# Attention with eight heads on two halves of the partitions, and the decay moved from the queries to the rows of the product

## The chip, the core and the metric

The kernel runs on one core of a Trainium2 chip. The core has a matrix engine (TensorE, in the profile PE, with its weight loads as PEld), a vector engine (VectorE, DVE), a scalar engine for functions (ScalarE, ACT), a general engine (GpSimd, POOL) and a queue that issues transfers (SyncE, SP). Matrix products are written to PSUM, eight banks of 512 float32 for each of the 128 partitions; everything else lives in SBUF. The metric is the device time of one execution in microseconds; lower is better. Times of a kernel differ between executions, so a median of several runs stands for it.

## What is computed

Two stages follow each other: a recurrent attention (mLSTM) with 4 batches, 8 heads, 768 steps and 40 values a head, and then a gated two-layer network over the 320 values of all heads, whose gate mixes the 768 positions.

```python
# attention; C, n and m start empty
m_new = max(f_gate[t] + m, i_gate[t])
f_stab, i_stab = exp(f_gate[t] + m - m_new), exp(i_gate[t] - m_new)
C = f_stab * C + i_stab * outer(v[t], k[t])
n = f_stab * n + i_stab * k[t]
y[t] = sigmoid(o_gate[t]) * (C @ q[t]) / max(abs(n @ q[t]), 1)
# network over x = all heads of y, 320 wide
h = max(x @ w_in, 0); u, v = halves of h (512 each)
v_s = w_spatial @ layer_norm(v) + b_spatial   # over the 768 positions
out = (u * v_s) @ w_out
```

## The kernel before

The 768 steps of a batch are cut into six blocks of 128 steps, and a block into two chunks of 64 (e = 0 and 1). There are 24 blocks in all, numbered n. Within a chunk the recurrence is written as products of matrices: keys and queries give scores, which are multiplied by a matrix of decays W and then by the values; what comes from earlier chunks is a state (40 x 41 a head: C and, as the 41st column, n) that meets the queries, times the decay since the chunk's start.

*The gates* (`gates`, L125 to L168) are done in two halves of 384 steps, on 32 partitions (4 x 8). Sums of gates go to DRAM (`scr_g`, `scr_a`, L141), and so does the decay since the chunk's start, `scr_e` (L161 to L165). They come back with the block's loads: `GM` and `AT`, whose product `ex` (L398) gives the exponents of W, and `Eb` (L378 to L381), the decay broadcast over 40 partitions.

*A block* has three parts. `att_load(n)` issues its loads on SP's queue: keys and queries `QK` (two transfers, L350 to L352; even chunk on partitions 64 to 103, odd on 0 to 39), `GM`, two of `Eb`, and two of `RH` (values, keys and output gates by time). `att1(n)` makes `ex`, the scores `s` (L361: for each head one product of 40 x 64 by 40 x 64 a chunk), W (ScalarE, L403), the product of scores and W into `KS` (VectorE, one instruction a chunk, L406), the queries times the decay, also into `KS` (GpSimd, L411, 40 x 512 a chunk), and the keys times the last column of W (GpSimd, L417). `att2(n)` makes the state's increments `dc` (L430, L432), carries the state from chunk to chunk with four VectorE instructions (L442 to L448; the state lies in rows of `RH` beside the values, alternately on the lower and the upper partitions), and then `pv` (L455, L456): one product a head and chunk whose 104 or 128 rows hold scores and decayed queries in one operand, and values and state in the other. VectorE divides and applies the output gate (L458 to L467), TensorE transposes (L476), and ScalarE and VectorE split the result into two float32r parts `xH` and `xL` (L478 to L481). A block's `att2` stands behind the `att1` of the next block and the loads of the one after.

*The network* follows: `a_v` (L494) makes v and its norm, `b_u` (L540) makes u (`pu`), mixes the positions (`pb`) and multiplies (GpSimd, L560), `c_out` (L565) writes the output. Weights come as float64 words and are split by `cvt` (L201), mostly on VectorE, and that for the first batch runs beside its attention. `seq` in line 54 is the written order of that first part: a token such as `q2` issues the loads of keys and queries of block 2, `s2` makes its scores, `h0` and `h1` are the halves of the gates, `A0` the loads of block 0, `T0` its `att1`, each `S` a block's attention, `C` a conversion. In later batches four or two steps of attention are placed between the `b_u` of each half (L633 to L644). From this order a scheduler, which simulates the engines, makes each engine's instruction stream; it places TensorE's work of other parts where it expects a wait.

PSUM is divided by kind (L90): `s` (two banks, `ex` and the scores), `dc`, `pv` and `px` (one each) and `pm` (three; `pu`, `pb`, `pc` and `a_v`).

## Time and profile before

| | us |
|---|---|
| median of 3 runs | 459.68 |
| lowest and highest run | 452.23, 465.68 |
| profiled execution, first to last instruction (span) | 441.9 |
| GpSimd busy in it | 173.6 |
| ScalarE busy in it | 156.1 |

The profiled execution has no time of its own beside its span. The runs' times include what lies before the first and after the last instruction; the median is 17.8 us above the span, the lowest run 10.3.

A row of a group of instructions reads: line, engine, operation, output from inputs by the program's names, shapes (for a matrix product rows*columns of the stationary operand, then the moving one), how many; then busy time in us and the mean of one in ns; then the engine's idle time just before them and what ended it. A float32 product shows as two records of TensorE, a float32r one as one. PEclk is the share of full speed that TensorE's clock was granted. A row of the timeline begins with the start and the duration, both in us, and merges neighbours of one kind. A row of a stage has the stage, its length, and the busy time of PE, PEld, DVE, ACT and POOL with the number of instructions.

### The profile page before, as it was taken

What the parts mean: (1) busy time and instruction counts of PE and PEld (TensorE: products, weight loads), DVE (VectorE), ACT (ScalarE), POOL (GpSimd) and SP (SyncE); (2) the same over time, 40 slices, a digit from 0 to 9 for tenths busy, and PEclk for the clock granted to TensorE, in tenths of its full rate; (3) what the DMA queues carried; (4) which work ended last, traced back from release to release, by engine and by line L of the source; (5) the groups of instructions that cost most, each with busy time, mean ns of one, the idle gap of its engine ahead of it and who ended that gap; (6) DMA issues with size and microseconds to landing.
All of it is one profiled execution on the core that took longest, in us unless ns stands there. A gap on an engine that the chain in (4) does not pass through costs nothing.

```text
span 441.9 us, 9266 instructions
## 1 busy us (share of the span) xinstructions
PE 402.6 (91%) x3648; PEld 331.9 (75%) x3648; DVE 249.8 (57%) x532; ACT 156.1 (35%) x372; POOL 173.6 (39%) x180
## 2 busy tenths in 40 slices
PE   3459969999898899999999997999999999999996
PEld 3337646678696788977888886677889887799895
DVE  6189967897899985234325465743355664322121
ACT  3144324547333242255422221267112315722211
POOL 4066541577654443236324033465242301633010
PEclk9999999988988998999999996999999999999999
DMA  7975428354055474000302242320024000000101
GB/s 182 201 207 178 133 51 234 110 137 106 20 171 143 113 196 136 0 15 16 91 1 60 93 107 77 92 60 31 30 61 130 8 3 0 32 15 1 45 0 47
DMA packets 18412, 36.83 MB, mean 83 GB/s; under 512 B 4176, under 2 KB 9040, under 8 KB 18368
## 3 DMA queue, kind: packets, MB, share of 16 engines
q1 hardware_dynamic: 14448, 31.43, 26.1%
q10 hardware_dynamic: 3504, 4.03, 2.6%
q0 software_dynamic: 416, 0.76, 0.9%
q8 instruction: 29, 0.48, 0.5%
q14 instruction: 15, 0.12, 0.1%
HBM read 31.79 MB, written 4.42 MB: 82 GB/s over the span
## 4 chain that ended last, share of the span: by engine, by line
PE 71%; DVE 12%; DMA 10%; issue 3%; ACT 2%; SPq 1%; POOL 1%; ACTq 0%; DVEq 0%; POOLq 0%
PE pu L547 12%; PE pb L553 9%; PE pb L555 7%; PE pb L554 7%; PE pv L456 4%; PE pc L571 4%; PE s L361 3%; PE pv L455 3%; PE pc L573 3%; DMA QK<-in_qk 3%; PE pc L572 3%; DMA RH<-in_vk 3%; DMA scr_g<-gp 2%; PE px L476 2%; DVE x L467 1%
## 5 line engine op out<-in xcount | busy, mean ns | idle before, releaser
L411 POOL TENSOR_TENSOR KS<-QK,Eb 40x512 f32<-40x512 f32 x44 | 59.2, 1345 | 69.5 <-DMA Eb<-scr_e 31.3
L560 POOL TENSOR_TENSOR g<-g,u 128x384 f32<-128x384 f32 x32 | 32.6, 1023 | 104.6 <-DVE g L559 89.0
L553 PE MATMUL pb<-wsH,vH 128*128 128x384 f32 x192 | 70.1, 365 | 3.4 <-ACT u L549 2.1
L554 PE MATMUL pb<-wsL,vH 128*128 128x384 f32 x192 | 66.0, 344 | 0.0
L555 PE MATMUL pb<-wsH,vL 128*128 128x384 f32 x192 | 65.9, 346 | 0.0
L361 PE MATMUL s<-QK 40*64 40x64 f32 x768 | 42.8, 255 | 13.3 <-DMA QK<-in_qk 9.7
L361 PEld LDWEIGHTS s<-QK 40*64 40x64 f32 x768 | 34.7, 162 | 22.8 <-DMA QK<-in_qk 10.8
L559 DVE TENSOR_TENSOR g<-pb,bsp 128x384 f32<-128x384 f32 x32 | 17.7, 556 | 53.3 <-PE pb L555 53.0
L553 PEld LDWEIGHTS pb<-wsH,vH 128*128 128x128 f32 x192 | 37.3, 194 | 9.2 <-issue 4.8
L455 PE MATMUL pv<-RH,KS 104*64 104x41 f32 (+1 forms) x384 | 40.1, 247 | 0.4 <-DVE x L465 0.4
L532 POOL TENSOR_TENSOR vL<-v,vH 128x512 fp32r<-128x512 f32 x24 | 31.0, 1292 | 20.8 <-DVE v L531 15.2
L456 PE MATMUL pv<-RH,KS 128*64 128x41 f32 x384 | 37.8, 246 | 1.2 <-DVE RH L443 0.6
L554 PEld LDWEIGHTS pb<-wsL,vH 128*128 128x128 f32 x192 | 37.5, 195 | 0.1
L555 PEld LDWEIGHTS pb<-wsH,vL 128*128 128x128 f32 x192 | 37.1, 194 | 0.2
L549 ACT ACTIVATE u<-pu 128x384 f32<-128x384 f32 x32 | 15.7, 489 | 60.9 <-PE pu L547 53.2
L547 PE MATMUL pu<-xH,wiL 128*128 128x384 f32 (+1 forms) x96 | 36.6, 382 | 0.0
L456 PEld LDWEIGHTS pv<-RH,KS 128*64 128x64 f32 x384 | 30.1, 150 | 8.1 <-issue 3.3
L455 PEld LDWEIGHTS pv<-RH,KS 104*64 104x64 f32 (+1 forms) x384 | 31.0, 150 | 6.7 <-issue 3.2
L547 PE MATMUL pu<-xH,wiH 128*128 128x384 f32 x96 | 34.9, 363 | 0.3 <-ACT ot L575 0.3
L406 DVE TENSOR_TENSOR KS<-s,W 64x512 f32<-64x512 f32 x48 | 32.9, 686 | 2.8 <-PE s L361 1.2
L562 DVE TENSOR_TENSOR big<-g,big 128x384 fp32r<-128x384 f32 x32 | 19.3, 605 | 25.9 <-ACT big L561 25.8
L413 ACT ACTIVATE RH<-RH 128x320 f32<-128x320 f32 x24 | 11.3, 470 | 61.2 <-DMA RH<-in_vk 57.5
(326 smaller groups left out, 863.7 us busy)
## 6 DMA issues: line engine op xcount, KB each, us to landing
RH<-in_vk SPq DMA_DIRECT2D x48, 242.0 KB
QK<-in_qk SPq DMA_DIRECT2D x48, 160.0 KB
Eb<-scr_e SPq DMA_DIRECT2D x48, 80.0 KB
out<-ot ACTq DMA_DIRECT2D x24, 160.0 KB
big<-in_w_sp SPq DMA_DIRECT2D x12, 192.0 KB
w<-in_w_in SPq DMA_DIRECT2D x8, 256.0 KB
w<-in_w_out SPq DMA_DIRECT2D x4, 320.0 KB
w<-in_w_rem SPq DMA_DIRECT2D x2, 256.0 KB
```

The lines of the kernel that those rows point to most:

```text
L361: nc.tensor.matmul(s[64 - p0:128 - p0, h], QK[p0:p0 + D, 0, h], QK[p0:p0 + D, 1, h], start=True, stop=True)
L406: nc.vector.tensor_tensor(out=ks[r, e], in0=s[r], in1=W[r], op=ALU.mult)
L411: eng(K["q" + "eo"[e] + ("0" if b == 0 else "")]).tensor_tensor(out=ks[r, e], in0=QK[r, 1], in1=Eb[r], op=ALU.mult)
L455: nc.tensor.matmul(pv[0:64, h], ks[0:ke, 0, h], v0[0:ke, h], start=True, stop=True)
L456: nc.tensor.matmul(pv[64:128, h], ks[:, 1, h], v1[:, h], start=True, stop=True)
L532: marks["v%d" % (b * NB + k)] = eng(K["vl0"] if b == 0 else K["vl"]).tensor_tensor(out=vL, in0=v, in1=vH.bitcast(F32), op=ALU.subtract)
L547: nc.tensor.matmul(pu, w, x, start=i == 0, stop=i == len(terms) - 1)
L553: nc.tensor.matmul(pb, vH[:, cd], wsH[hf][:, s], start=s == 0, stop=False)
L554: nc.tensor.matmul(pb, vH[:, cd], wsL[hf][:, s], start=False, stop=False)
L555: nc.tensor.matmul(pb, vL[:, cd], wsH[hf][:, s], start=False, stop=s == NB - 1)
L560: marks["m%d" % ((b * 2 + hf) * 4 + d)] = nc.gpsimd.tensor_tensor(out=g, in0=g, in1=u, op=ALU.mult)
L562: marks["g%d" % ((b * 2 + hf) * 4 + d)] = nc.vector.tensor_tensor(out=gL, in0=g, in1=gH.bitcast(F32), op=ALU.subtract)
```

## The change

Heads 0 to 3 now have keys and queries on partitions 0 to 39 and heads 4 to 7 on 64 to 103, both chunks each, in four buffers (`QKS`). The scores of a block use all four 64x64 quarters of the array in turn (`TILES`), in one PSUM buffer of two banks; `KS` is written by one VectorE instruction over 128 partitions. The decayed queries and `Eb` are gone. Scores times values (`XI`, 64 rows) and raw queries times state (`XD`, 40 rows, again over the four quarters) are separate products. The second is multiplied by the decay of its row (`ET`) and added to the first, by two VectorE instructions, before the division. The state has buffers of its own (`ST`), four heads on each half of the partitions, so a step is 104 x 164 in place of 40 x 328; in a batch's first block a buffer of zeros stands for it. `dc` shares the two banks of `XD` with the state's product.

The gates give `ET` (decay by time, through three TensorE transposes a half) and `DEC` (the chunk's whole decay on all partitions, through a product with a loaded matrix `pick`); `scr_e` is gone. `RH` is one transfer a block. `ex` and `px` move to the three banks `pm`. In `seq`, `id` goes ahead of `h0`, and `q3`, `s3` and `rh` are dropped. `keep_warm`, which was called with counts of zero, and choices among engines that were fixed are removed.

```diff
-    'seq': ('h0', 'id', 'q0', 'gm0', 'ks', 'q1', 's0:v1', 's1', 'q2', 'q3', 'at0', 'rh', 's2', 's3', 'La', 'h1', 'A0', ...
+    'seq': ('id', 'h0', 'q0', 'gm0', 'ks', 'q1', 's0:v1', 's1', 'q2', 'at0', 's2', 'La', 'h1', 'A0', ...
...
+    BANKS = {"s": 1, "pm": 3}
 
     def bank(shape, name, kind):
-        tag, n = cfg[kind]
-        t = ps.tile(shape, F32, name=name, tag=tag, bufs=n)
-        return t
+        return ps.tile(shape, F32, name=name, tag=kind, bufs=BANKS[kind])
...
+    ET = const.tile([128, NB, BH], F32, name="ET")
+    DEC = const.tile([128, 2 * NB, 16], F32, name="DEC")
+    pick = const.tile([128, 144], F32, name="pick")[0:BH]
...
+        nc.gpsimd.dma_start(out=pick, in_=a["pick"])
...
-            gv = gz.rearrange("p (k e t) -> p k e t", e=2, t=L)
-            ev = ez.rearrange("p (k e t) -> p k e t", e=2, t=L)
-            for e in range(2):
-                nc.scalar.activation(out=ev[:, :, e], in_=gv[:, :, 1 - e], func=AF.Exp)
-            eng(K["dqg"]).dma_start(out=scr_e[cs].rearrange("c p t -> p c t"), in_=ez.rearrange("p (c t) -> p c t", t=L))
+            nc.scalar.activation(out=ez, in_=gz, func=AF.Exp)
+
+            pe = bank([128, 512], "pe", "pm")
+            for i in range(NB // 2):
+                nc.tensor.transpose(pe[:, i * BH:(i + 1) * BH], ez[:, i * 128:(i + 1) * 128], ident[0:BH, 0:BH])
+            nc.vector.tensor_copy(out=ET[:, z * 3:z * 3 + 3], in_=pe[:, 0:3 * BH].rearrange("p (k c) -> p k c", c=BH))
+            dg = wk.tile([128, NB, 16], F32, name="dg", tag="dg", bufs=1)[0:BH]
+            nc.vector.tensor_tensor(
+                out=dg, in0=ez.rearrange("p (c t) -> p c t", t=L)[:, :, L - 1:L].broadcast_to([BH, NB, 16]),
+                in1=pick[:, 0:16].unsqueeze(1).broadcast_to([BH, NB, 16]), op=ALU.mult)
+            pd = bank([128, 512], "pd", "pm")[:, 0:NB * 16]
+            nc.tensor.matmul(pd, pick[:, 16:144], dg.rearrange("p c x -> p (c x)"), start=True, stop=True)
+            nc.vector.tensor_copy(out=DEC[:, cs], in_=pd.rearrange("p (c x) -> p c x", x=16))
...
+    NKS, NRH, NQK, NST = 3, 3, 4, 4
     VW, KW = H * E, H * D
-    KS = [const.tile([128, 2, H, L], F32, name=f"KS{j}") for j in range(NKS)]
-    RH = [const.tile([128, 2 * VW + 2 * KW], F32, name=f"RH{j}") for j in range(NRH)]
-
-    def rh_v(t, e):
-        o = e * (VW + 2 * KW)
-        return t[:, o:o + VW].rearrange("p (h d) -> p h d", h=H)
+    HH = H // 2
+    HI = 64 + D
...
+    KS = [const.tile([128, H, L], F32, name=f"KS{j}") for j in range(NKS)]
+    RH = [const.tile([128, VW + 2 * KW], F32, name=f"RH{j}") for j in range(NRH)]
+    QKS = [const.tile([128, 2, 2, HH, L], F32, name=f"QK{j}") for j in range(NQK)]
+    ZS = const.tile([128, HH, E], F32, name="ZS")
+    XI = ps.tile([128, 512], F32, name="XI", tag="XI", bufs=1)
+    ST = [const.tile([128, HH, E], F32, name=f"ST{j}") for j in range(NST)]
+    XD = ps.tile([128, 2, 512], F32, name="XD", tag="XD", bufs=1)
+
+    def rh_v(t):
+        return t[:, 0:VW].rearrange("p (h d) -> p h d", h=H)
...
+    def xv(hf):
+        return XD[:, hf, 0:HH * E].rearrange("p (h d) -> p h d", h=HH)
+
+    def dcv(e):
+        return XD[:, e, HH * E:2 * HH * E].rearrange("p (h d) -> p h d", h=HH)
...
-        for t in KS:
-            nc.gpsimd.memset(t[32:64, 1], 0.0)
-
-    def init_rh():
-        for t in RH:
-            nc.gpsimd.memset(rh_v(t, 1)[32:64], 0.0)
+        nc.gpsimd.memset(ZS, 0.0)
+        nc.vector.memset(XD[32:64], 0.0)
...
-        if 2 <= n < K["npre"]:
-            QK = early_keys.tile([128, 2, H, L], F32, name="QK%d" % n)
-        else:
-            QK = ld.tile([128, 2, H, L], F32, name="QK", tag="QK", bufs=2)
-        for e, p0 in ((0, 64), (1, 0)):
-            loads["a%d" % n] = (nc.scalar if n < K["npre"] and K["qkq"] else nc.sync).dma_start(out=QK[p0:p0 + D], in_=a["qk"][b, k, e])
+        QK = QKS[n % NQK]
+        for hf in range(2):
+            loads["a%d" % n] = nc.sync.dma_start(out=QK[64 * hf:64 * hf + D].rearrange("p e w h t -> p (e w h t)"), in_=a["qk"][b, k, hf])
...
+    TILES = ((0, 0), (1, 1), (0, 1), (1, 0))
...
+        s = bank([128, 2, 512], "s", "s")
+        for j in range(HH):
+            for hf, e in TILES:
+                r = slice(64 * hf, 64 * hf + D)
                 nc.tensor.matmul(
-                    s[64 - p0:128 - p0, h], QK[p0:p0 + D, 0, h], QK[p0:p0 + D, 1, h], start=True, stop=True)
+                    s[64 * e:64 * e + 64, hf, j * L:(j + 1) * L], QK[r, e, 0, j], QK[r, e, 1, j], start=True, stop=True)
         sc[n] = s
...
-        Eb = ld.tile([128, H, L], F32, name="Eb", tag="Eb")
-        for e in range(2):
-            nc.sync.dma_start(
-                out=Eb[64 * e:64 * e + D], in_=scr_e[2 * k + e, b * H:(b + 1) * H].unsqueeze(0).broadcast_to([D, H, L]))
         rh = RH[n % NRH]
-        for e in range(2):
-            nc.sync.dma_start(out=rh[64 * e:64 * e + 64, e * VW:e * VW + VW + 2 * KW], in_=a["vk"][b, k, e])
-        tl[n] = (QK, gm, Eb, rh)
+        nc.sync.dma_start(out=rh, in_=a["vk"][b, k])
+        tl[n] = (QK, gm, rh)
...
+        ex = bank([128, H * L], "ex", "pm")
...
-        nc.scalar.activation(out=W, in_=ex, func=AF.Exp)
-        for e in range(2):
-            r = slice(64 * e, 64 * e + 64)
-            nc.vector.tensor_tensor(out=ks[r, e], in0=s[r], in1=W[r], op=ALU.mult)
-        for e, p0 in ((0, 64), (1, 0)):
-            if k == 0 and e == 0:
-                continue
-            r = slice(p0, p0 + D)
-            eng(K["q" + "eo"[e] + ("0" if b == 0 else "")]).tensor_tensor(out=ks[r, e], in0=QK[r, 1], in1=Eb[r], op=ALU.mult)
+        nc.scalar.activation(out=W.rearrange("p h t -> p (h t)"), in_=ex, func=AF.Exp)
+        nc.vector.tensor_tensor(
+            out=ks.rearrange("p (g h) t -> p g (h t)", g=2), in0=s[:, :, 0:HH * L], in1=W.rearrange("p (g h) t -> p g (h t)", g=2), op=ALU.mult)
...
+        kt, v = rh_k(rh), rh_v(rh)
+        s0, s1, s2 = (ST[(2 * n + i) % NST] for i in range(3))
+        if k == 0:
+            s0 = ZS
...
-        dc = bank([128, H, E], "dc", "dc")
+        for e in range(1 if last else 2):
+            r = slice(64 * e, 64 * e + 64)
+            for j in range(HH):
+                for hf in range(2):
+                    h = hf * HH + j
+                    nc.tensor.matmul(dcv(e)[64 * hf:64 * hf + D, j], kt[r, h], v[r, h], start=True, stop=True)
+
+        def step(e, old, new):
+            if old is None:
+                nc.vector.tensor_copy(out=new[0:HI], in_=dcv(e)[0:HI])
+                return
+            tmp = wk.tile([128, HH, E], F32, name="tmp", tag="tmp", bufs=K["tmp"])
+            nc.vector.tensor_tensor(out=tmp[0:HI], in0=old[0:HI], in1=DEC[0:HI, 2 * k + e, b * HH:(b + 1) * HH].unsqueeze(2).broadcast_to([HI, HH, E]), op=ALU.mult)
+            nc.vector.tensor_tensor(out=new[0:HI], in0=dcv(e)[0:HI], in1=tmp[0:HI], op=ALU.add)
+
+        step(0, s0 if k else None, s1)
+        if not last:
+            step(1, s1, s2)
+
+        def inter(e, h):
+            hf, j = divmod(h, HH)
+            r = slice(64 * hf, 64 * hf + D)
+            nc.tensor.matmul(xv(hf)[64 * e:64 * e + 64, j], QK[r, e, 1, j], (s1 if e else s0)[r, j], start=True, stop=True)
+
+        xi = XI[:, 0:H * E].rearrange("p (h d) -> p h d", h=H)
         for h in range(H):
-            nc.tensor.matmul(dc[0:D, h], kt[0:64, h], v0[0:64, h], start=True, stop=True)
-            if not last:
-                nc.tensor.matmul(dc[64:64 + D, h], kt[64:128, h], v1[64:128, h], start=True, stop=True)
-        lo, hi = slice(0, D), slice(64, 64 + D)
-
-        def decay(r):
-            return Eb[r, :, L - 1:L].broadcast_to([D, H, E])
-
-        if k == 0:
-            nc.vector.tensor_copy(out=v1[lo], in_=dc[lo])
-        else:
-            tmp = wk.tile([128, H, E], F32, name="tmp", tag="tmp", bufs=K["tmp"])
-            eng(K["tp0"][0] if b == 0 else "v").tensor_tensor(out=tmp[lo], in0=v0[hi], in1=decay(hi), op=ALU.mult)
-            nc.vector.tensor_tensor(out=v1[lo], in0=dc[lo], in1=tmp[lo], op=ALU.add)
-        if not last:
-            nv0 = rh_v(RH[(n + 1) % NRH], 0)
-            tmp = wk.tile([128, H, E], F32, name="tmp", tag="tmp", bufs=K["tmp"])
-            eng(K["tp0"][1] if b == 0 else "v").tensor_tensor(out=tmp[hi], in0=v1[lo], in1=decay(lo), op=ALU.mult)
-            nc.vector.tensor_tensor(out=nv0[hi], in0=dc[hi], in1=tmp[hi], op=ALU.add)
-        pvf = bank([128, 512], "pv", "pv")
-        pv = pvf[:, 0:H * E].rearrange("p (h d) -> p h d", h=H)
-        if n < 6:
-            keep_warm(pvf[:, 0:128], K["we"][n])
-        ke = 64 if k == 0 else 64 + D
-        for h in range(H):
-            nc.tensor.matmul(pv[0:64, h], ks[0:ke, 0, h], v0[0:ke, h], start=True, stop=True)
-            nc.tensor.matmul(pv[64:128, h], ks[:, 1, h], v1[:, h], start=True, stop=True)
+            for e in range(2):
+                r = slice(64 * e, 64 * e + 64)
+                nc.tensor.matmul(xi[r, h], ks[r, h], v[r, h], start=True, stop=True)
+        for j in range(HH):
+            for hf, e in TILES:
+                inter(e, hf * HH + j)
+        xs = wk.tile([128, H, E], F32, name="xs", tag="xs", bufs=2)
+        nc.vector.tensor_tensor(
+            out=xs.rearrange("p (g h) d -> p g h d", g=2), in0=XD[:, :, 0:HH * E].rearrange("p g (h d) -> p g h d", h=HH),
+            in1=ET[:, k, b * H:(b + 1) * H].rearrange("p (g h) -> p g h", g=2).unsqueeze(3).broadcast_to([128, 2, HH, E]), op=ALU.mult)
+        nc.vector.tensor_tensor(out=xs, in0=xi, in1=xs, op=ALU.add)
...
+        px = bank([128, 3, 128], "px", "pm")
...
+        t = t.reshape(B, 2, H // 2, NB, 2, L, D)
+        return t.transpose(0, 3, 1, 6, 4, 2, 5)
+    r["qk"] = c(np.stack([qk(inp["k"]), qk(inp["q"])], 5)).reshape(B, NB, 2, D, 2 * 2 * (H // 2) * L)
...
+    p = np.zeros((BH, 144), np.float32)
+    i = np.arange(BH)
+    p[i, i // H * (H // 2) + i % (H // 2)] = 1.0
+    p[:, 16:] = np.arange(128)[None] // 64 == (i % H // (H // 2))[:, None]
+    r["pick"] = p
```

76 lines of the change are left out of this document (14 added, 62 removed).

## Prediction, made before the changed kernel ran

> **What bounds the kernel now.** I read the page first, then the busy time by stages, then the groups of instructions with their shapes kept apart, and last the timeline at single places.
>
> ```profile
> span 441.9 us, 9266 instructions
> ...
> PE 402.6 (91%) x3648; PEld 331.9 (75%) x3648; DVE 249.8 (57%) x532; ACT 156.1 (35%) x372; POOL 173.6 (39%) x180
> ...
> PE 71%; DVE 12%; DMA 10%; issue 3%; ACT 2%; SPq 1%; POOL 1%; ACTq 0%; DVEq 0%; POOLq 0%
> ```
>
> The third row is the chain that ended last: TensorE holds 71% of it, VectorE and DMA 22%. These lie in different stages:
>
> ```profile
> core 0: us, PE busy (x) PEld busy (x) DVE busy (x) ACT busy (x) POOL busy (x), PEclk, DMA share, GB/s
> 0.00:24.00 24.00, 9.24 (x129) 8.15 (x129) 10.70 (x22) 6.54 (x15) 6.10 (x17) 1.00 0.79 190
> 24.00:190.00 166.00, 150.22 (x1535) 117.59 (x1536) 132.04 (x278) 65.62 (x159) 83.12 (x81) 0.95 0.45 127
> 190.00:442.00 252.00, 243.11 (x1986) 206.17 (x1985) 107.02 (x234) 83.93 (x198) 84.34 (x84) 0.99 0.15 45
> ```
>
> Until 24 us the DMA engines are 79% busy and nearly everything waits for loads and gates. From 24 to 190 us the first batch's attention and the conversion of the weights share VectorE: 132.0 of 166 us busy, more than in the later stage, and the clock falls to 0.95 because TensorE pauses. From 190 us TensorE is the bound: 243.1 of 252 us, with VectorE at 42%. So work taken from GpSimd, VectorE and DMA is worth something before 190 us, and after it only where TensorE stops for it.
>
> The 24 blocks of attention cost, by line and shape:
>
> ```profile
> L411 POOL TENSOR_TENSOR KS<-QK,Eb 40x512 f32<-40x512 f32 x44 | 59.2, 1345 | 69.5 <-DMA Eb<-scr_e 31.3 <-PE pv L456 23.1 <-DMA GM<-scr_g 6.7
> L361 PE MATMUL s<-QK 40*64 40x64 f32 x768 | 42.8, 255 | 13.3 <-DMA QK<-in_qk 9.7 <-ACT W L403 3.2 <-DVE KS L406 0.3
> L456 PE MATMUL pv<-RH,KS 128*64 128x41 f32 x384 | 37.8, 246 | 1.2 <-DVE RH L443 0.6 <-DVE RH L439 0.6
> ...
> L406 DVE TENSOR_TENSOR KS<-s,W 64x512 f32<-64x512 f32 x48 | 32.9, 686 | 2.8 <-PE s L361 1.2 <-ACT W L403 0.7 <-PE pv L456 0.3
> ...
> L467 DVE SCALAR_TENSOR_TENSOR x<-RH,x 128x320 f32<-128x320 f32 x24 | 21.3, 889 | 0.5
> ...
> L465 DVE TENSOR_TENSOR x<-pv,den 128x320 f32<-128x320 f32 x24 | 11.7, 488 | 0.6
> ...
> L447 DVE TENSOR_TENSOR tmp<-RH,Eb 40x328 f32<-40x328 f32 x20 | 11.3, 564 | 0.6
> ...
> L442 DVE TENSOR_TENSOR tmp<-RH,Eb 40x328 f32<-40x328 f32 x20 | 10.9, 544 | 0.6
> ...
> L448 DVE TENSOR_TENSOR RH<-dc,tmp 40x328 f32<-40x328 f32 x20 | 10.1, 503 | 0.6
> L443 DVE TENSOR_TENSOR RH<-dc,tmp 40x328 f32<-40x328 f32 x20 | 9.6, 481 | 3.3 <-PE dc L432 2.8 <-PE dc L430 0.2
> ...
> L224 DVE TENSOR_TENSOR rest<-rest,ex 128x256 f32<-128x256 f32 x6 | 5.8, 959 | 0.3
> ...
> L458 DVE TENSOR_SCALAR den<-pv 128x8 f32<-128x8 f32 x24 | 3.9, 163 | 17.1 <-PE pv L456 16.8
> ...
> L233 DVE TENSOR_TENSOR wiL<-bits,rest 128x256 fp32r<-128x256 f32 x8 | 3.8, 474 | 0.1
> ```
>
> **The change part by part.** *GpSimd (L411).* The decayed queries are no longer made: 44 products of 1345 ns, 59.2 us of GpSimd's 173.6, and the wait for Eb with them. What that is worth lies on VectorE. L467 reads two SBUF operands; L465 has the same 320 elements, but one operand from PSUM:
>
> ```profile
> L467 DVE SCALAR_TENSOR_TENSOR x<-RH,x x24: 474/560/2821, 41.2 to 369.7; 128x320 f32<-128x320 f32 x24
> ...
>   PE px L476: 4.8, 4
> ...
> 264.10 2.60 POOL L411 TENSOR_TENSOR KS<-QK,Eb 40x512 f32<-40x512 f32 x2 [6.70 <-DMA GM<-scr_g]
> ...
> 265.79 2.28 DVE L467 SCALAR_TENSOR_TENSOR x<-RH,x 128x320 f32<-128x320 f32 x1
> 266.66 0.98 POOL L560 TENSOR_TENSOR g<-g,u 128x384 f32<-128x384 f32 x1
> 267.61 1.06 POOL L417 TENSOR_TENSOR RH<-RH,W 128x320 f32<-128x320 f32 x1
> ...
> 268.22 0.66 PE L476 MATMUL px<-ident,x 128*128 128x128 f32 x2 [3.28 <-DVE x L467]
> ...
> 268.00:274.40 6.40, 6.18 (x20) 4.90 (x21) 3.03 (x7) 1.79 (x5) 0.67 (x1) 0.50 0.51 131
> ```
>
> The fastest L467 takes 474 ns, the slowest 2821. At 265.79 us it starts while L411 runs (to 266.70), L560 follows without a gap (to 267.64), and 0.43 us after that L467 ends: it did its work when GpSimd's two had ended. TensorE has waited 3.28 us for it, and then runs 6.4 us at a granted clock of 0.50. All waits of TensorE for L467 come to 4.8 us. GpSimd's L560 and L417 stay, so I count the 3.28 and a third of the other 1.5 us as gone, 3.8, and with the half clock (6.4 us at 0.50 loses 3.2 us) **−7 us**. Bounds: 0, if L560 and L417 alone hold VectorE as long; −8.0 if all goes.
>
> *VectorE.* KS is one instruction over 128 partitions for two over 64: −686 ns. The state becomes 104 x 164 for 40 x 328. A small product takes 163 ns at 8 elements (L458) and 488 at 320 (L465), so 1.04 ns an element; 164 elements come to 0.325 us, and four of them 1.30 for 544 + 564 + 503 + 481 = 2.09: −0.79. Two products of 328 elements are added (xs, and the sum with XI), each near L448's 503: +1.01. That is −0.47 us a block. L467's own share by stage:
>
> ```profile
> 24.00:190.00 166.00, 8.73 (x13) 0.95 0.45 127
> 190.00:442.00 252.00, 12.60 (x11) 0.99 0.15 45
> ```
>
> So 13 blocks lie before 190 us and 11 behind. The 13 save 6.1 us by the shapes, and 8.73 − 13 x 0.474 = 2.6 us on L467. The conversions wait in the same way (L224 takes 959 ns where L233 of equal size takes 474): −2.9 for these six, and I estimate as much again for the others. Together 14.5 of the 132.0 us. How much reaches the end? VectorE is busy 80% of that stage, TensorE 90%. I take two thirds, **−10 us**. Bounds: 0 (something else sets the order) and −22 (166 x 14.5 / 132 = −18, and half of what the clock of 0.95 costs, 8 us, comes back).
>
> *TensorE.* Scores keep their 32 records a block (fp32 products show as two each), now spread over four 64x64 tiles. The product with values keeps 32 records, over 64 rows; 32 records are added where raw queries meet the state. dc is the same. At one place the old kernel already has four tiles at work, since scores there use the two off-diagonal tiles and dc the two diagonal ones:
>
> ```profile
> 254.84 0.97 PE L361 MATMUL s<-QK 40*64 40x64 f32 x26
> ...
> 255.64 0.23 PE L361 MATMUL s<-QK 40*64 40x64 f32 x2
> ...
> 255.66 0.21 PE L430 MATMUL dc<-RH 64*40 64x41 f32 x1
> 255.66 0.21 PE L432 MATMUL dc<-RH 64*40 64x41 f32 x1
> ...
> 255.70 0.22 PE L361 MATMUL s<-QK 40*64 40x64 f32 x1
> ```
>
> Two tiles: 26 scores in 0.97 us less a last one of 0.22, 0.029 us a record. Four tiles: from 255.64 to 255.70 four records start, 0.015 each. So scores fall from 0.93 to 0.47 us and the added product costs 0.47: **0**. Bounds: +0.93 a block if four are no faster than two, +10 over the eleven blocks after 190 us; −3 (0.3 a block) if the array, held in one mode through attention, saves the pauses at pv's beginning and end. The Trainium skill speaks against me here: "TensorE: Matmul & The Clock Gate", section "Back-to-back issue gap", has matmuls of up to 64 columns no closer than about 25 ns. By that, an estimate from the page, scores would take 0.8 us, the added product 0.8, and the sum would be 0.67 us a block worse; the rows with 0.015 us disagree.
>
> *DMA and the start.* Eb's 48 broadcasts and scr_e go; RH becomes one transfer with the same bytes; q3 and its scores go; ident moves ahead of the gates' loads, and pick is issued on GpSimd's queue ahead of its gm and at loads.
>
> ```profile
> QK<-in_qk SPq DMA_DIRECT2D x48, 160.0 KB
> ...
> Eb<-scr_e SPq DMA_DIRECT2D x48, 80.0 KB
> ...
> scr_e<-big SPq DMA_DIRECT2D x2, 48.0 KB
> ...
>   DMA AT<-scr_a: 4.9, 1
> ```
>
> TensorE's first ex (L398) waits 4.9 us for AT. On SP's queue two QK, two scr_e and one Eb stand ahead of AT's load: 320 + 96 + 80 = 496 KB, 2.6 us at 190 GB/s, and their issues. Ident's and pick's issues give some 0.4 us back. **−3 us**; bounds 0 (scr_g and scr_a keep AT late) and −6. The gates gain three transposes, a matmul and three small VectorE products a half (96 elements, 0.26 us each by the slope above); VectorE idles then, so nothing, and at most +2 if the second half's products stand behind a wait for TensorE.
>
> *PSUM.* ex and px now share three banks with the MoE products; XD holds dc and the state product, so dc of the next block waits until xs is read; scores have one buffer, so those of blocks 1 and 2 wait for KS of the one before. I take **+2 us**; bounds 0 and +8 (a third of a microsecond a block).
>
> Sum: −7 − 10 + 0 − 3 + 0 + 2 = −18 us, a span of 423.9. The runs' median is 459.68, so 17.8 us lie around the profiled span; I leave them alone: 459.7 − 18 = **441.7 us**.
>
> **The rivals.** *The early relief is hidden.* Then the order of SP's loads and of the conversions bounds the first batch, not VectorE; DMA's 10% of the chain speaks for it, VectorE's 80% against. The start's gain shrinks to 1: −7 − 1 + 2 = −6, 454 us. *Four tiles run no faster than two*: −18 + 10, 452 us; only the short stretch at 255.64 speaks against it. The Trainium skill's 25 ns (same page and section) would be a weaker form: 11 x 0.67 = 7, 449 us by that estimate. *Slower: TensorE waits for the state.* Half of the added product needs the state after the first chunk, and the banks that it shares with dc bar it until VectorE's state steps have read them; they bar dc of the next block until xs is read. Unfilled, that is 4 x 0.325 us plus one KS ahead in the queue, 2.0 us in each of 24 blocks: +48 − 18, 490 us. It makes the kernel slower by 2% from 1.1 us a block on ((18 + 9) / 24). Against it: the old kernel has the same round trip from dc to pv, and L456 waits 1.2 us for it in all, since MoE products fill it.
>
> **How the numbers follow.** The forecast, 426 to 450, has 0.62; the hidden relief 0.17; two-tile speed 0.08; the wait for the state 0.13. 2%, 9 us, is about what a measurement here can tell from no change: faster lies below 450.5. Faster takes the forecast and a quarter of the two-tile case (which may come with a larger relief), 0.64; same the rest of that case and the hidden relief, 0.23; slower 0.13. The range 426 to 456 holds the forecast and the two other faster cases but for some 0.07 at their ends, and leaves out the slow one: 0.80.
>
> **What would show it.** Right: no L411 and GpSimd near 114 us; L467 near 500 ns on average; VectorE near 225 us; sixteen products of a block with the state inside about 0.5 us; a first ex near 21 us; the stage that ends now at 190 us ending some 10 us earlier. Wrong: TensorE idle before the state product or before dc, more half-clock stretches after 190 us, or the first batch ending when it does now with VectorE idler.

## The result, and the profile after

The changed kernel is slower: 476.62 us (four runs, 474.01 to 479.77) against 455.96 for the kernel before on the same chip (447.94 to 465.68). The ratio is 1.057, 95% interval 1.045 to 1.069. (All ratios here compare undisturbed runs of both kernels, so they are not the quotients of the medians.) The prediction was 441.7 us and faster.

The page of the changed kernel, in the same lines as before, and its slices of the granted clock:

```profile
span 473.5 us, 10635 instructions
...
PE 393.5 (83%) x4426; PEld 333.5 (70%) x4426; DVE 219.6 (46%) x563; ACT 157.2 (33%) x370; POOL 112.6 (24%) x132
...
PEclk9999966558757998779998899989997989999999
...
PE 59%; DVE 17%; DMA 10%; ACT 6%; POOL 3%; issue 3%; SPq 0%; POOLq 0%; ACTq 0%; DVEq 0%
```

The work went where the change meant it to go: GpSimd from 173.6 to 112.6 us, VectorE from 249.8 to 219.6, TensorE from 402.6 to 393.5. But the span less TensorE's busy time, its idle time, went from 39.3 to 80.0 us. Nothing became a bound; TensorE stops more. By stages, as before (columns: stretch, length, busy times, clock, DMA):

```profile
0.00:24.00 24.00, 3.84 (x42) 2.99 (x42) 15.07 (x37) 8.46 (x20) 5.53 (x14) 1.00 0.92 256
24.00:190.00 166.00, 128.46 (x1800) 106.54 (x1800) 97.55 (x250) 59.49 (x141) 39.66 (x44) 0.79 0.29 90
190.00:474.00 284.00, 261.23 (x2586) 223.93 (x2584) 107.01 (x277) 89.27 (x210) 67.37 (x74) 0.94 0.13 42
```

In the stage from 24 us VectorE is now 59% busy (it was 80%) and TensorE 77% (it was 90%). The engine that was relieved is idler, and so is the one that was to profit. The first network product of batch 1, which ended that stage at 189.0 us, starts at 208.4; from there to the end it takes 265.2 us for 252.9. So 19 us are lost before it (4 of them by the first ex, which starts at 28.1 us for 23.8) and 12 behind it.

What TensorE waited for (in all, times, longest):

```profile
PE s L361 <- DVE KS L390: 17.8, 11, 5.7
PE ex L384 <- DMA AT<-scr_a: 14.0, 1, 14.0
PE px L461 <- DVE x L454: 8.6, 13, 1.7
PE XD L414 <- POOL RH L395: 7.4, 7, 4.4
...
PE XD L431 <- DVE ST L422: 4.6, 4, 2.2
```

The first row is new: before, scores waited 0.3 us for KS. They have one buffer now, and KS needs W, which needs ex. So the row says that ex comes late, or that one buffer is too few; it can't tell which. The last row is the wait for the state, which was my slower rival: 4.6 us, not 48.

The groups, shapes apart (busy, mean ns, idle before):

```profile
L437 PE MATMUL XI<-RH,KS 64*64 64x41 f32 x768 | 40.8, 259 | 0.3
...
L390 DVE TENSOR_TENSOR KS<-s,W 128x512 f32<-128x512 f32 x24 | 16.5, 688 | 11.8 <-ACT W L389 10.2 <-PE s L361 1.6
L421 DVE TENSOR_TENSOR tmp<-ST,DEC 104x164 f32<-104x164 f32 x40 | 16.1, 401 | 0.9
...
L422 DVE TENSOR_TENSOR ST<-XD,tmp 104x164 f32<-104x164 f32 x40 | 12.8, 320 | 0.6
L445 DVE TENSOR_TENSOR xs<-XI,xs 128x328 f32<-128x328 f32 x24 | 11.9, 496 | 0.5
...
L454 DVE SCALAR_TENSOR_TENSOR x<-RH,x 128x320 f32<-128x320 f32 x24 | 11.7, 488 | 0.5
```

L454, the old L467, takes 488 ns on average (889 before). Most instruction prices were right: 688 ns for KS (686 expected), 496 and 494 for the added products (503), 488 for L454 (500); the state's first step takes 401 for 325.

**Where ex went.** Until the first px, the order on TensorE is the clearest sign of what changed. Before (timeline; start, duration, line, shape):

```profile
23.77 0.77 PE L398 MATMUL ex<-GM,AT 84*128 84x512 f32 x1 [4.94 <-DMA AT<-scr_a]
25.22 0.79 PE L398 MATMUL ex<-GM,AT 84*128 84x512 f32 x1 [0.69 <-ACT W L403]
30.20 0.76 PE L398 MATMUL ex<-GM,AT 84*128 84x512 f32 x1 [1.16 <-DMA GM<-scr_g]
37.00 0.80 PE L398 MATMUL ex<-GM,AT 84*128 84x512 f32 x1
39.39 0.77 PE L398 MATMUL ex<-GM,AT 84*128 84x512 f32 x1 [0.34 <-ACT wsH L282]
43.48 0.69 PE L476 MATMUL px<-ident,x 128*128 128x128 f32 x2
```

Changed:

```profile
28.12 1.19 PE L384 MATMUL ex<-GM,AT 84*128 84x512 f32 x2 [14.03 <-DMA AT<-scr_a]
...
46.00 0.69 PE L461 MATMUL px<-ident,x 128*128 128x128 f32 x2
46.48 0.42 PE L462 MATMUL px<-ident,x 128*64 128x128 f32 x1
46.55 0.77 PE L384 MATMUL ex<-GM,AT 84*128 84x512 f32 x1
```

Five blocks' ex ran ahead of the first px; now two do, and the third stands directly behind px of the first block. That px ends a long chain (products, state, division, output gate). The reading that suggests itself is that banks go out in the order in which the code asks for them: two ex and one px hold the three shared banks, so the third ex comes behind px, and W, KS and the next scores behind it. The experiments test what the division costs; the order itself is read from timelines.

**A correction to how I read the clock.** The view of one tile shows how long the scores' records take, here in two stretches of the kernel before, until 79.9 us and behind it (count; minimum, median, maximum ns; first and last start):

```profile
L361 PE MATMUL s<-QK x86: 311/311/367, 40.4 to 77.3; 40*64 40x64 f32 x86
L361 PE MATMUL s<-QK x74: 218/218/267, 80.4 to 91.2; 40*64 40x64 f32 x74
```

The granted clock by the page of the kernel before, in slices of 11.05 us:

```profile
PEclk9999999988988998999999996999999999999999
```

The scores' records of the changed kernel:

```profile
L361 PE MATMUL s<-QK x96: 311/311/367, 31.5 to 51.6; 40*64 40x64 f32 x96
L361 PE MATMUL s<-QK x32: 218/218/267, 74.7 to 75.1; 40*64 40x64 f32 x32
```

A record takes 311 ns in the stretches granted 0.50 and 218 at 1.00. In the kernel before it takes 311 from the first one to 77 us, although the page shows full clock there: the trace's first clock record lies at 79.9 us, and the page counts time without a record as full. So the kernel before runs at half clock until 79.9 us and for 24.1 us later, 104.0 in all; the changed one until 56.6 us and for 102.8 later, 159.4. With that the spans can be taken apart. Idle is what no TensorE record covers after the first ex; the half clock's cost is TensorE's busy time in those stretches times 1 − 174/320, since products of 128x384 start 174 ns apart at full and 320 at half clock. The ends of TensorE's records are modelled, and the same products come out at 342.5 to 352.8 us of work in the last three rows, so that column is good to some 10 us only:

| kernel | first ex | idle after it | cost of half clock | work at full clock | span |
|---|---|---|---|---|---|
| before | 23.8 | 24.6 | 31.7 | 361.8 | 441.9 |
| changed | 28.1 | 55.7 | 47.2 | 342.5 | 473.5 |
| e14, below | 27.5 | 30.9 | 32.9 | 352.8 | 444.1 |
| e17, below | 23.1 | 35.1 | 30.9 | 351.0 | 440.0 |

The new computation is thus no more work for TensorE, and perhaps some 10 us less: by the same working e8 (new) comes to 357.0 and e3 (old) to 354.9. Against the kernel before, the changed one has 31 us more of stops, and 16 us more from half clock. That these stops are what halves the clock is not shown.

### The profile page after: what moved, and what is told of

It is laid out like the page before. It is cut to its first block, busy times and chain, and to the rows that moved or that the text cites. A ratio compares the mean times of both kernels' runs of the same rounds, so it can differ in the third digit from the quotient of the medians.

```text
span 473.5 us, 10635 instructions
## 1 busy us (share of the span) xinstructions
PE 393.5 (83%) x4426; PEld 333.5 (70%) x4426; DVE 219.6 (46%) x563; ACT 157.2 (33%) x370; POOL 112.6 (24%) x132
## 4 chain that ended last, share of the span: by engine, by line
PE 59%; DVE 17%; DMA 10%; ACT 6%; POOL 3%; issue 3%; SPq 0%; POOLq 0%; ACTq 0%; DVEq 0%
PE pu L530 11%; PE pb L536 8%; PE pb L537 7%; PE pb L538 7%; DMA RH<-in_vk 5%; PE pc L554 4%; PE pc L555 3%; PE pc L556 3%; DMA QK<-in_qk 3%; DMA w<-in_w_in 2%; DVE x L454 2%; PE px L461 2%; DVE x L452 2%; DVE xs L445 1%; POOL g L543 1%
## 5 line engine op out<-in xcount | busy, mean ns | idle before, releaser
L538 PE MATMUL pb<-wsH,vL 128*128 128x384 f32 x192 | 64.4, 339 | 0.0
L361 PE MATMUL s<-QK 40*64 40x64 f32 x768 | 23.2, 263 | 29.7 <-DVE KS L390 17.8
L361 PEld LDWEIGHTS s<-QK 40*64 40x64 f32 x768 | 18.9, 169 | 33.7 <-DVE KS L390 19.8
L437 PE MATMUL XI<-RH,KS 64*64 64x41 f32 x768 | 40.8, 259 | 0.3
L437 PEld LDWEIGHTS XI<-RH,KS 64*64 64x64 f32 x768 | 36.0, 168 | 4.5 <-issue 3.8
L530 PE MATMUL pu<-xH,wiL 128*128 128x384 f32 (+1 forms) x96 | 38.3, 399 | 0.0
L530 PE MATMUL pu<-xH,wiH 128*128 128x384 f32 x96 | 37.0, 386 | 0.4 <-ACT ot L558 0.3
L393 ACT ACTIVATE RH<-RH 128x320 f32<-128x320 f32 x24 | 11.2, 469 | 68.0 <-DMA RH<-in_vk 68.0
L554 PE MATMUL pc<-woH,big 128*128 128x320 f32 x96 | 32.3, 342 | 0.0
L555 PE MATMUL pc<-woL,big 128*128 128x320 f32 x96 | 30.7, 326 | 0.0
L545 DVE TENSOR_TENSOR big<-g,big 128x384 fp32r<-128x384 f32 x32 | 18.2, 571 | 26.5 <-ACT big L544 26.1
L414 PE MATMUL XD<-RH 64*40 64x41 f32 x704 | 21.0, 231 | 11.3 <-POOL RH L395 7.4
L556 PE MATMUL pc<-woH,big 128*128 128x320 f32 x96 | 29.8, 326 | 0.0
```

Of the source, the lines that this page charges most:

```text
L361: nc.tensor.matmul(s[64 * e:64 * e + 64, hf, j * L:(j + 1) * L], QK[r, e, 0, j], QK[r, e, 1, j], start=True, stop=True)
L414: nc.tensor.matmul(dcv(e)[64 * hf:64 * hf + D, j], kt[r, h], v[r, h], start=True, stop=True)
L437: nc.tensor.matmul(xi[r, h], ks[r, h], v[r, h], start=True, stop=True)
L530: nc.tensor.matmul(pu, w, x, start=i == 0, stop=i == len(terms) - 1)
L538: nc.tensor.matmul(pb, vL[:, cd], wsH[hf][:, s], start=False, stop=s == NB - 1)
L554: nc.tensor.matmul(pc, gH[:, c], woH[:, d], start=d == 0, stop=False)
```

## The experiments

Two theories stood at the start: ScalarE's order (a tanh that waits for its load stands ahead of W, and with it KS and the scores wait), and the division of PSUM's banks. All results in one table; times are medians, and "ahead" is the number of ex that start before the first px.

| kernel | us | ratio to before | 95% interval | ahead |
|---|---|---|---|---|
| changed | 476.6 | 1.057 | 1.045 to 1.069 | 2 |
| e1 tanh behind W | 470.7 | 1.042 | 1.031 to 1.052 | 2 |
| e2 four buffers for RH | 471.4 | 1.046 | 1.035 to 1.057 | 2 |
| e3 old, banks as changed | 504.4 | 1.116 | 1.106 to 1.127 | 2 |
| e4 old, written order as changed | 455.5 | 1.012 | 1.005 to 1.018 | 5 |
| e5 old, px shared | 468.2 | 1.044 | 1.033 to 1.054 | 5 |
| e6 old, ex shared | 462.5 | 1.028 | 1.008 to 1.047 | 3 |
| e7 old, one scores buffer | 457.2 | 1.019 | 1.011 to 1.028 | 3 |
| e8 new, ex own bank | 461.4 | 1.028 | 1.022 to 1.034 | 4 |
| e9 new, px own bank | 451.1 | 1.002 | 0.995 to 1.009 | 3 |
| e10 new, two score halves | 475.7 | 1.060 | 1.045 to 1.075 | 2 |
| e11 new, gates before weights | 475.8 | 1.058 | 1.049 to 1.066 | 2 |
| e12 e8, e10 and e11 together | 464.6 | 1.032 | 1.023 to 1.042 | 4 |
| e13 new, px beside scores | 451.5 | 1.002 | 0.998 to 1.006 | 3 |
| e14 e13 and ex own bank | 445.4 | 0.982 | 0.974 to 0.990 | 5 |
| e15 e9 and two score halves | 480.1 | 1.059 | 1.050 to 1.067 | 3 |
| e16 old, two network banks | 475.0 | 1.048 | 1.037 to 1.059 | 6 |
| e17 e14, gates before weights | 441.8 | 0.975 | 0.971 to 0.980 | 5 |
| e18 old, banks as e14 | 473.9 | 1.047 | 1.037 to 1.056 | 3 |

### ScalarE's order, buffers, banks, written order (e1 to e4)

e1 puts each tanh behind the W of its block:

```diff
-        nc.scalar.activation(out=W.rearrange("p h t -> p (h t)"), in_=ex, func=AF.Exp)
+        w_done = nc.scalar.activation(out=W.rearrange("p h t -> p (h t)"), in_=ex, func=AF.Exp)
...
-        nc.scalar.activation(out=so, in_=so, func=AF.Tanh, scale=0.5)
+        with tc.issue_after(w_done.ins):
+            nc.scalar.activation(out=so, in_=so, func=AF.Tanh, scale=0.5)
```

> The changed kernel, with the tanh of block n queued on ScalarE behind W of block n; nothing else is edited, though the scheduler plans anew. Theory A (ScalarE's order): the changed kernel puts the tanh of block n+1 ahead of W of block n, so W waits for the RH transfer of block n+1, KS and the next scores wait for W, TensorE pauses and its clock halves. Then this edit takes most of the loss back: 476 to 455-463 us, TensorE's wait for KS (17.8 us) falls below 8, mean clock 0.89 to 0.94 or more. Rival B (one buffer of scores): scores of n+1 wait for KS of n in any order of ScalarE; then 470-480 us, and the wait for KS stays near 18 us. Rival C (the start and the written order): 470-480 us as well.

e2 gives RH a fourth buffer, and takes one each from KS and ST to make room:

```diff
-    NKS, NRH, NQK, NST = 3, 3, 4, 4
+    NKS, NRH, NQK, NST = 2, 4, 4, 3
```

> The changed kernel with four RH buffers in place of three, so that the load of a block waits for x of one block earlier; to make room KS has two buffers and the state three. ScalarE's order stays (tanh of n+1 ahead of W of n). Theory A: the order does harm only because the RH transfer lands late, so 476 to 460-468 us, and ScalarE's wait for RH (68 us) halves. Rival B: 472-480 us, TensorE's wait for KS stays.

e3 is the old computation, loads and written order, with the changed kernel's division of the banks; two banks stay unused in it:

```diff
-        dict(s=("s", 2), dc=("dc", 1), pv=("pv", 1), px=("px", 1), pm=("pm", 3)),
+        dict(s=("s", 1), dc=("dc", 1), pv=("pv", 1), px=("pm", 3), pm=("pm", 3)),
...
-        s = bank([128, H, L], "s", "pm" if n < min(3, K["npre"]) else "s")
+        s = bank([128, H, L], "s", "s")
...
-        ex = bank([128, H, L], "ex", "s" if n >= K["npre"] else K["exb"])
+        ex = bank([128, H, L], "ex", "pm")
```

> The kernel before, computation and loads unchanged, with the changed kernel's sharing of PSUM: ex and px share the three banks pm with the network's products, scores have one buffer and none in advance in pm. Its ScalarE order turns over in the same way. Theory A and rival B (both are effects of the PSUM division): 455 to 468-485 us, with GpSimd's load of the old kernel on top. If the loss comes from the new computation instead (two products, the extra VectorE work, the array mode): 450-462 us.

e4 is the old kernel with only the written order of the change (ident first, q3 and s3 no longer in advance; 'rh' stays, since the old kernel needs it):

```diff
-    'seq': ('h0', 'id', 'q0', 'gm0', 'ks', 'q1', 's0:v1', 's1', 'q2', 'q3', 'at0', 'rh', 's2', 's3', 'La', ...
+    'seq': ('id', 'h0', 'q0', 'gm0', 'ks', 'q1', 's0:v1', 's1', 'q2', 'at0', 'rh', 's2', 'La', ...
```

> The kernel before with the changed written order alone: ident ahead of the gates, no early loads and scores of block 3. Rival C (the start): 460-466 us, first ex 3 us or more later. Theories A and B: 452-460 us.

e1 and e2 are 6 and 5 us lower by medians, with intervals that overlap the changed kernel's. In e1 the scores still wait 16.0 us for KS (17.8 before it), so the tanh was not what made W late: that theory falls. e3 answers instead. The old computation takes 504.4 us where the kernel before took 451.3 on the same chip, 53 us by medians and 52 by the ratio, by nothing but the banks, and it shows the changed kernel's pattern. TensorE's waits in e3:

```profile
PE ex L398 <- DMA AT<-scr_a: 14.9, 1, 14.9
PE s L361 <- DVE KS L406: 14.6, 11, 3.8
PE pv L455 <- DVE x L465: 12.2, 9, 2.7
PE px L476 <- DVE x L467: 10.8, 11, 3.2
```

and e3's timeline at the first px:

```profile
43.56 0.69 PE L476 MATMUL px<-ident,x 128*128 128x128 f32 x2
44.05 0.42 PE L477 MATMUL px<-ident,x 128*64 128x128 f32 x1
44.12 0.77 PE L398 MATMUL ex<-GM,AT 84*128 84x512 f32 x1
```

The same wait for KS, and again the third ex directly behind the first px. With the same things sharing banks the new computation is 27.8 us faster than the old (476.6 against 504.4). So the change holds a gain and a larger loss. e4 puts the written order at 1.2% (0.5 to 1.8), about 5 us.

### Which part of the division (e5 to e8)

e5 shares px alone, e6 ex alone (with the early scores in their own two buffers), e7 gives ex a bank of its own and leaves scores one; e8 is the changed kernel with a bank for ex, taken from the network's three.

```diff
 e5
-        dict(s=("s", 2), dc=("dc", 1), pv=("pv", 1), px=("px", 1), pm=("pm", 3)),
+        dict(s=("s", 2), dc=("dc", 1), pv=("pv", 1), px=("pm", 3), pm=("pm", 3)),
 e6
-        ex = bank([128, H, L], "ex", "s" if n >= K["npre"] else K["exb"])
+        ex = bank([128, H, L], "ex", "pm")
 e7
+        dict(s=("s", 1), ex=("ex", 1), dc=("dc", 1), pv=("pv", 1), px=("px", 1), pm=("pm", 3)),
 e8
-    BANKS = {"s": 1, "pm": 3}
+    BANKS = {"s": 1, "pm": 2, "ex": 1}
```

> The old kernel with px taken from the three banks of the network's products instead of its own; nothing else differs. All three parts of the new division of PSUM together (ex shared, px shared, one buffer for scores) cost the old computation 50 us (504.4 against 451.3). Theory X, that px waiting for a bank of the network (and the network for px) is the main part: 470 to 490 us, TensorE's wait px <- and the wait for x grow. Rival theories (E: ex; S: scores): 450 to 460 us.

> The old kernel with ex taken from the three banks of the network's products, and all scores from the two buffers that ex and scores shared before (so scores have one buffer more than in the new division); px keeps its own bank. Theory E, that ex (and with it the gates' exponential) now waits for a bank of the network and comes late: 470 to 495 us, with TensorE's wait for KS (s <- KS) or ex's own wait for banks at 10 us or more. If px or the single scores buffer is the cause: 450 to 462 us.

> The old kernel with a bank of its own for ex and a single bank for scores (none of the early scores in the network's banks); px keeps its own bank and the network its three. Theory S, that the single buffer takes away the run ahead of the scores: 470 to 495 us, with s <- KS (the scores of the next block wait until VectorE has multiplied those of this one) at 14 us or more, as in the new kernel's 17.8. If sharing ex or px is the cause: 450 to 462 us.

> The new kernel with ex in a bank of its own and two banks, instead of three, for the network's products and px. Theory E, that ex behind the network's results costs the new kernel about 20 us of its 25: 455 to 465 us. If px in the network's banks or the number of the network's banks is what hurts, two banks make it worse: 480 to 500 us. If the single scores buffer is the cause: 470 to 480 us, unchanged.

No part carries the loss alone: px 4.4%, ex 2.8%, one buffer of scores 1.9%, 9.1 together, and 11.6% when they meet. With intervals of one or two per cent on each part, that they cost more together than apart is not shown. My expectations of 20 us and more for one part were all too high, and so all three single theories fall in that form. In the changed kernel a bank for ex returns 15 us although the network pays with one of its own; scores, still with one buffer, then wait 2.5 us for KS instead of 17.8:

```profile
PE s L361 <- DVE KS L390: 2.5, 2, 2.0
```

So that wait was ex's lateness, not the buffer.

In e5 ex runs five blocks ahead, as before, and yet 4.4% are lost. The timelines show a second queue. In the kernel before, the first product of the network (`pv__494`, made by `a_v`) starts ahead of the second block's px; in e5 it stands directly behind it:

```profile
46.31 0.80 PE L505 MATMUL pv__494<-wiH,xH 128*128 128x512 f32 x1
...
51.95 0.69 PE L476 MATMUL px<-ident,x 128*128 128x128 f32 x2 [0.19 <-DVE x L467]
```

```profile
56.24 0.69 PE L476 MATMUL px<-ident,x 128*128 128x128 f32 x2
56.72 0.42 PE L477 MATMUL px<-ident,x 128*64 128x128 f32 x1
56.79 0.78 PE L505 MATMUL pv__494<-wiH,xH 128*128 128x512 f32 x1
```

So it is in all kernels of this document: the nine in which px shares the network's banks (changed, e1, e2, e3, e5, e8, e10, e11, e12) have no network product ahead of the second px, and the other eleven have two to eight records of it there. px in the network's banks holds back the network as well as ex. What share of the loss this has was not measured.

### px, the scores' buffer, the start (e9 to e12)

e9 gives px the bank instead of ex. e10 lets blocks take the two halves of the scores' banks in turn. There the scores of block 2 are written over those of block 0 before these are used, so the first values of its output are others; its operations are those of the changed kernel, each with its shape. e11 starts the early weights behind the store of scr_a. e12 joins e8, e10 (with the same overwritten scores) and e11.

```diff
 e9
-    BANKS = {"s": 1, "pm": 3}
+    BANKS = {"s": 1, "pm": 2, "px": 1}
 e10
-        s = bank([128, 2, 512], "s", "s")
+        s = SS[:, :, 256 * (n % 2):256 * (n % 2) + 256]
 e11
-'L0', 'L1', 'L2', 'C0', 'C2', 'L3', 'L4', 'L5',
+'L0:ap', 'L1:ap', 'L2:ap', 'C0', 'C2', 'L3:ap', 'L4:ap', 'L5:ap',
```

> The new kernel with px, instead of ex, in a bank of its own, and two banks for the network's products and ex. With ex in its own bank and two for the network and px it took 461.4, against 476.6. Theory D, that what hurts is any of the two standing in one queue for banks with the network, so that the network's late results hold back the attention of the next batch: 455 to 468 us, as with ex, since px shared cost the old kernel 4.4% and ex shared 2.8%. Theory E, that only ex matters in the new kernel, where one buffer of scores waits for it: 470 to 490 us.

> The new kernel with two buffers for scores in the same two banks: blocks take the first and the second 256 columns of each in turn, since one block's scores fill only 256 of 512; all else as in the new kernel. TensorE's waits s <- KS (17.8 us in the new kernel) must go. Theory S, that the single buffer carries the loss (stops of TensorE halve its clock): 455 to 465 us. Theory D, that sharing banks with the network does: 470 to 477 us; the waits move to ex or px.

> The new kernel with the six early loads of weights written to start behind the store of the gates' last scratch (scr_a), so that the gates' scratch is not queued behind 12 weight transfers on SP. The first ex should start at about 24 us as before (28.1 in the new kernel) and the wait ex <- AT fall from 14.0 to 10 us or less. Theory that the start is worth what it lasts: 471 to 473 us. Rival, that the weights come late instead and the network of the first batch waits: 476 us or more.

> The new kernel with all three: ex in a bank of its own (two for the network and px), two halves for scores, and the gates' scratch ahead of the weights. Theory D with S and the start: each gives its part, 461.4 less 4 for the start less 5 to 10 for the scores: 447 to 453 us, level with before or a little faster. If the own bank of ex had already taken what the halves would give: 456 to 460 us.

e9 takes the whole loss away: 451.1 us, level with before and below what either of its theories allowed (455 or more). e10 did not become the test that it was meant to be. Its wait for KS should have gone and is still there:

```profile
PE SS L362 <- DVE KS L391: 19.8, 13, 3.7
```

From block 3 on no scores of e10 start before KS of the block before theirs has ended, so the two halves did not work as two buffers. That one buffer is not the main cause rests on e8 and e9 instead: both have one, and scores wait 2.5 and 2.0 us for KS. In e11 the first ex does start early, at 24.1 us, and the time stays. TensorE's longest waits in e11 (in all, times, longest):

```profile
PE px L462 <- DVE x L455: 13.4, 17, 1.6
PE s L362 <- issue: 11.5, 3, 5.2
PE s L362 <- DVE KS L391: 11.2, 12, 1.5
PE ex L385 <- DMA AT<-scr_a: 10.2, 1, 10.2
```

AT's wait fell by 3.8 us, px's grew by 4.8: still only two ex run ahead of the first px, so an earlier start is waited for elsewhere. e12 (464.6) gains nothing over e8 (461.4) and misses both of its forecasts, 447 to 453 and 456 to 460; as in e10, no scores behind those written ahead start before KS of the block before theirs has ended.

### Is the gain of the computation there? (e13 to e18)

e13 puts px into the columns that scores leave free in their two banks, so that it takes no bank from anyone; e14 adds a bank for ex, with two for the network. In both (and in e17), scores of blocks 1 and 2 are no longer written ahead, in e15 those of block 2.

```diff
 e13
+    SS = ps.tile([128, 2, 512], F32, name="SS", tag="SS", bufs=1)
...
-        s = bank([128, 2, 512], "s", "s")
+        s = SS[:, :, 0:256]
...
-        px = bank([128, 3, 128], "px", "pm")
+        px = SS[:, 0, 256:512].rearrange("p (j c) -> p j c", j=2)
+        px2 = SS[:, 1, 256:384]
 e14 (with e13)
-    BANKS = {"s": 1, "pm": 3}
+    BANKS = {"pm": 2, "ex": 1}
 e15 (e9 and)
+        s = SS[:, :, 256 * (n % 2):256 * (n % 2) + 256]
 e16 (old)
+        dict(s=("s", 2), dc=("dc", 1), pv=("pv", 1), px=("px", 1), pm=("pm", 2)),
 e17: e14 with e11's order of the early weights
 e18 (old; ex as in e7)
+        dict(s=("s", 1), ex=("ex", 1), dc=("dc", 1), pv=("pv", 1), px=("px", 1), pm=("pm", 2)),
```

> The new kernel with px in the columns of the scores' two banks that scores leave free (256 of 512 in each), so that ex and the network keep all three shared banks; the scores of blocks 1 and 2 are no longer written ahead of the first batch. Theory D (px behind the network's results is what cost the 25 us, and the computation gains what was forecast): 438 to 447 us, since the network has one bank more than in e9 (451.1). Rival theory G, the computation gains nothing once px is free: 449 to 456 us. Rival theory E, ex in the shared banks still hurts: 455 us or more.

> As e13, with ex in a bank of its own and two for the network alone, so that nothing of the attention waits for a result of the network. If ex shared still costs (E): 435 to 445 us, faster than e13. If two banks are too few for the network by itself: slower than e13, 450 us or more. Theory G: 449 to 456 us.

> e9 (px in its own bank, two for the network and ex) with two buffers for scores, in halves of the same two banks. In e10 two halves at the new division of the rest were worth nothing (475.7 against 476.6). If they are worth something only where px is free: 440 to 447 us; if nothing here either: 448 to 455 us, as e9.

> The old kernel with two banks for the network's products instead of three, nothing shared that was not. The price of the third bank: if it is what keeps e9 from the forecast gain, 460 to 470 us; if two are enough for the network when nothing else stands in its queue, 452 to 458 us.

> e14 (nothing shared with the network) with the six early loads of weights behind the store of scr_a, as in e11. If the 4 us of the late first ex reach the end now that no bank is waited for: 440 to 443 us. If they are hidden by later work, as in e11: 444 to 447 us.

> The old computation at the division of e14: one bank each for scores, ex, dc, pv and px, two for the network. If the new computation gains by itself what e3 against the new kernel shows at the other division (504.4 to 476.6, 28 us): 468 to 482 us against e14's 445. If e14's place for px and not the computation is what makes it fast: 445 to 455 us.

e14 is the first that is faster than before, and e17 is 2.5% faster (2.0 to 2.9). Its page (busy time, granted clock in 40 slices) and its longest wait of TensorE:

```profile
PE 385.7 (88%) x4426; PEld 321.7 (73%) x4426; DVE 220.7 (50%) x563; ACT 157.5 (36%) x370; POOL 112.9 (26%) x132
...
PEclk9999855555999889999999999999999999999999
```

```profile
PE ex L386 <- DMA AT<-scr_a: 9.1, 1, 9.1
```

Five ex run ahead again, TensorE's idle time by the page is 54.3 us (80.0 in the changed kernel), and the clock is full from the 16th slice (165 us) on. e17 is below e14 by medians (441.8 against 445.4), but on another chip and with intervals of the ratios that overlap, so that the earlier start reaches the end is likely and not shown.

e18 prices the computation a second time: 473.9 for the old one at a division near e14's (px has a bank of its own), 445.4 for the new, 28.5 us, as 27.8 at the other division. This is not what the change is worth with all eight banks in use: the old computation leaves two unused in e3 and one in e18, which the new one needs for XI and XD. e18 with its unused bank given to the network is e7, at 457.2; against that e14 leads by some 3.7% (ratios 1.019 and 0.982). e16 shows a price above both of its forecasts (460 to 470, 452 to 458): the old kernel with two banks for the network and nothing else changed takes 475.0, so its third bank is worth some 22 us. That may be why e9 and e13 stop level with before, but e13, with three banks shared with ex, is no faster than e9 with two, so the two prices don't simply add.

e15 went against its expectation by 25 us and more. It has TensorE idle for 51.2 us after the first ex (e9: 33.4) and waits 16.1 us for x at px. As in e10, the halves did not work as two buffers (from block 2 on no scores start before KS of the block before theirs has ended), so this says nothing of a second buffer; where the loss comes from is open. The count of ex ahead is not the whole story either: e9 and e13 with three are faster than e8 with four, and e5 and e16 lose 4.4 and 4.8% with five and six. The order in which the engines' instructions are laid out is planned anew for each kernel, and some of these differences may be that; no run prices it alone.

## Why the prediction was wrong

The step that failed is "*PSUM.* … I take **+2 us**; bounds 0 and +8 (a third of a microsecond a block)". It measured +25.5 in the new computation for px alone (476.6 against 451.1 in e9, which gives px a bank and takes one from the network), +31 with ex apart too (445.4 in e14, which also writes fewer scores ahead), and some +52 in the old (e3). The fault lies in how it was priced: as a small stop in each block, when it is a place in a queue. One px in front holds back later ex, with W, KS and the scores behind them, and the network's products too; TensorE then stops for 31 us more and loses 16 us more to half clock. That the division of the banks makes the loss is shown; the split between the two queues is not. I had written down the three sharings in one sentence and not followed what stands behind what.

The other steps:

- *L467 and GpSimd, −7.* GpSimd 112.6 (114 forecast) and 488 ns (500) are right, but TensorE's waits for x did not go: 8.6 us in 13 stops for 4.8 in 4. The long stop of 3.28 us is gone, the longest is 1.7, and more short ones stand in its place. px's shared bank is not the whole reason: in e9, with a bank for px, the wait is 11.2 us in 8 stops, the longest 3.3. In e17 it is 1.9 us.
- *VectorE, −10.* 219.6 us (225). The state's steps cost 401 and 320 ns for my 325, the two added products 496 and 494 for 503, and the conversion L222 (before L224) 424 for 959, as forecast. The stage did not end 10 us earlier but 19 later.
- *TensorE, 0.* Right that four tiles work at a time: within a block the records of scores start 15.4 ns apart at full clock, for 30.4 with two (medians over the blocks). The Trainium skill's floor of about 25 ns ("TensorE: Matmul & The Clock Gate", section "Back-to-back issue gap") does not hold for them, which lie on different tiles. TensorE's work at full clock is 9 to 11 us less in e14 and e17 than before, in the changed kernel 19 (table above); with some 10 us of uncertainty, 0 was perhaps too high.
- *DMA and the start, −3.* The sign was wrong: first ex at 28.1 us, not 21, and 14.0 us of wait for AT. SP's queue has the weights' loads ahead of the gates' scratch; e11 and e17, which move them behind it, start at 24.1 and 23.1. The written order alone puts the old kernel's first ex at 26.5 us (e4) and costs 1.2%. The 496 KB were counted, what moved ahead of them was not.
- *The 17.8 us around the span.* They are not there: the changed kernel's profiled execution took 475.29 us with a span of 473.5, 1.8 around it. By the same 1.8 us the profiled execution of before took about 443.7, less than any of its runs beside these experiments (444.6 to 469.0). The sum of −18 should have been set against about 444 us for the span shown.

The part of the sum that stands for the computation, −7 −10 +0 −3 = −20, is near what e3 and e18 measure for it, −28, but with banks left unused on the old side, and its −3 had the wrong sign; how the 28 us split among GpSimd, VectorE and TensorE was not tried. So the terms are not confirmed by their sum, and that e17 takes 441.8 us, the forecast value, is luck.

Of the rivals, two-tile speed falls (15.4 ns against 30.4), and the hidden relief falls in its form (28 us with the same things sharing banks are not hidden). The slower one had the right sign and the wrong place: the state's product (L431) waits 4.6 us for VectorE's state steps, and dc (L414) 7.4 us for GpSimd's L395, which needs W; neither is a wait for XD's banks. That one shows in e17, where dc waits 3.3 us for xs. The forecast's own test, "TensorE idle before the state product or before dc, more half-clock stretches after 190 us", saw both parts: these waits, and 34 us of half clock after 190 us for 6.8 before.

## What to carry to other kernels

Before a change takes PSUM banks, write down for each bank who asks for it, in the order of the code, and find what stands behind the latest of them. If something that should run far ahead (here ex) shares banks with something that ends a long chain (px), its run ahead is cut, and so is that of the fill work (here the network's products) that asks behind px; the price is set by everything that hangs behind it, not by one short wait in each block. A bank whose columns are half empty can hold a second thing, if the lifetimes allow it: with px beside the scores and a bank for ex, the changed kernel went from 5.7% slower to 1.8% faster than before. It is not free: in e13 px waits 4.3 us for KS, which reads the scores, and scores 1.7 us for the reading of px, and in e13, e14 and e17 no product into these two banks overlaps an instruction that reads them.
